# An earlier request for half of w1, and two places in TensorE's first plan

## The chip, the cores and the metric

The kernel runs on one core of a Trainium2 chip. The metric is the device time of one execution in microseconds (us), as the median of several runs. The profile tells of one further execution, taken by the hardware profiler.

## The reference

The reference is a block-sorting attention followed by a mixture of experts.

```python
# attention: 4 batches, 8 heads, 768 rows of 64, in 8 blocks of 96 rows
for _ in range(5):                        # P = sort_net, (4, 8, 8, 8)
    P = exp(P - max(P, -1)); P /= sum(P, -1) + 1e-9; P /= sum(P, -2) + 1e-9
k_sorted = einsum('bhij,bhjcd->bhicd', P, k_blocks)     # v_sorted likewise
scores = q_block @ k_sorted_block.T / sqrt(64)          # inside each block
out = softmax(scores) @ v_sorted_block
# experts: x is that output as 3072 rows of 512; 8 experts, hidden width 1024
P = exp(x @ w_gate - max)
for _ in range(8):
    P /= P.sum(1) + 1e-9; P /= P.sum(0) + 1e-9; P *= 3072 / 8
out = sum_e P[:, e] * (relu(x @ w1[e]) @ w2[e])
```

## The kernel before

**Stages.** The first batch's attention runs by itself at the start. The attention of batches two to four is woven with expert 0 of the batch ahead, and the other seven experts follow. Matrix products run on TensorE in bf16 with f32 sums. ScalarE and VectorE empty its banks, GpSimd issues the loads that turn f32 into bf16 and does sums that need no bank.

**The sort.** P is balanced in five rounds, spread over 128 partitions, and multiplied with a mask into R (`Rt[bb]`), a 128 x 128 matrix for each head. `sort_values` (L144) multiplies R with the values, copies the products to `vs` and moves them to `vsbt` with eight transfers, one a block of rows (`vsb` in the profile). For the first batch block i goes out on SP, GpSimd and ScalarE in turn, so SP has blocks 0, 3 and 6. `keys` (L186) sorts the keys in the same way. R of the first batch is made on VectorE. R of the second batch is made on GpSimd by `build_r` (L130), in two instructions of four heads each, line L134.

**w1 of expert 0.** It is loaded in two halves by `half_w1` (L103): half 0 holds rows 0 to 255 of w1, so kk = 0 and 1 of the four steps over the inner dimension; half 1 holds kk = 2 and 3. Half 0 is asked for early. Half 1 is asked for on GpSimd between the two R instructions of the second batch (L461 to L464). Behind it GpSimd asks for the second batch's v, k and q and for w2 of expert 0 (L465, L466).

**The order of the work.** `pin` is the language's request to keep an instruction in the order in which the program names it. Everything on TensorE and GpSimd is pinned, and so is nearly all of the first batch on ScalarE and VectorE. The first batch's order is written out by hand in the string `PLAN0`, which `first_attention` (L306) walks through. A letter is a step, the first digit is the pair of heads, the second the half of the blocks:

- `k0`: sort the keys of pair 0 (L194, copies on VectorE L200). `s00`: scores of pair 0, half 0 (L218), and their exponentials on ScalarE (L232).
- `d00`: denominators, a product of the exponentials with ones (L243), and their reciprocal on VectorE (L246). `m00`: the mix with the sorted values (L256) and a multiply by the reciprocal on VectorE (L258). With a capital letter (`D`, `M`) the VectorE part is put off until a step `f`.
- `t00`: turn the result (L282) and copy it to `xtT` (L287), the input of the experts.
- `w2`: two matmuls into a bank that nobody reads (`unread`, L423).
- `e0`: the first two of eight pieces of expert 0's hidden layer, kk = 0 and 1, in two banks (L358). `e1` is kk = 2, `e2` is kk = 3 and the relu. So e1 is the first reader of half 1 of w1. `h0`: a further piece of the hidden layer (L368). `l0`, `l3`: logits (L300).

**The banks.** The first stage takes its results from seven banks. Which bank a step gets is settled when the program is built: the one that comes free first. So a step can have to wait for whoever reads the bank's earlier content.

Of the kernel before, what the change touches and what calls it, by code (L numbers as in the profile page):

```python
# [20 lines left out]
def mkap(t, dims, off=0):  # L21
    return bass.AP(tensor=t.tensor, offset=t.offset + off, ap=dims)
# [3 lines left out]
def kernel(  # L26
# [11 lines left out]
    nc = tc.nc  # L38
# [33 lines left out]
    def load_batch(bb, parts):  # L72
        for d, name in ((vt, "vt"), (kt, "kt"), (qt, "qt")):
            d[bb] = kvp.tile([128, 8, 384], BF16, name=name, bufs=2)
        load_rest(bb, parts)
# [16 lines left out]
    def load_w2(e):  # L92
        w2t[e] = (wq if e else wcp).tile([128, 8, Dm], BF16, name="w2e")
        pin(nc.gpsimd.dma_start(out=w2t[e],
                                in_=moe_w2[e].rearrange("(fb k) f -> k fb f", k=128)))
# [7 lines left out]
    def half_w1(h):  # L103
        pin(nc.gpsimd.dma_start(
            out=w1t[0][:, 2 * h:2 * h + 2],
            in_=moe_w1[0, 256 * h:256 * h + 256].rearrange("(kk k) f -> k kk f", k=128)))
# [23 lines left out]
    def build_r(bb, eng, n):  # L130

        Rt[bb] = perp.tile([128, 8, 8, 16], BF16, name=f"R{bb % 2}")
        for h in range(0, 8, n):
            ins = eng.tensor_tensor(  # L134
                out=mkap(Rt[bb], [Rt[bb].ap[0], [16, 8 * n], [1, 16]], off=h * 128),
                in0=mkap(Pb, [Pb.ap[0], [1, 8 * n], [0, 16]], off=(bb * 8 + h) * 8),
                in1=mkap(mask16, [mask16.ap[0], [0, 8 * n], [1, 16]]),
                op=ALU.mult)
            if eng is nc.gpsimd:
                pin(ins)  # L140
            yield


    def sort_values(bb, bank, n=8, h0=0):  # L144
        for h in range(h0, n):
            vps = bank([128, 384], F32)
            pin(nc.tensor.matmul(vps, Rt[bb][:, h].rearrange("p i c -> p (i c)"),  # L147
                                 vt[bb][:, h, :], start=True, stop=True))
            (nc.vector.tensor_copy if bb == 0 and h in (3, 5, 7) or bb == 1 and h % 2 else
             nc.scalar.copy)(  # L150
                vs[:, :, h, 0:64], vps.rearrange("p (kk d) -> p kk d", d=64))
            if h % 2:
                yield

        for i in range(NB if n == 8 else 0):
            eng = ((nc.sync, nc.gpsimd, nc.scalar)[i % 3] if bb == 0 else
                   nc.gpsimd if i % 2 else nc.sync)
            (pin if bb == 0 else lambda ins: ins)(eng.dma_start(
                out=mkap(vsbt[bb % 2], [[VW, 96], [1, 520]], off=i * 520),
                in_=vs[16 * i:16 * i + 16].rearrange("p kk h d -> p kk (h d)")))  # L160
# [3 lines left out]
    def queries(bb, hp, bank):  # L164

        qps = bank([128, 6, 128], BF16)
        if bb < 2:

            for kk in range(6):
                for h in range(2):  # L170
                    pin(nc.tensor.matmul(qps[64 * h:64 * h + 64, kk, :],
                                         qt[bb][:, 2 * hp + h, kk * 64:kk * 64 + 64],
                                         Ibig, is_transpose=True, start=True, stop=True))
        else:
            qr = sp.tile([128, 6, 2, 64], BF16, name="qr", bufs=2)
            nc.gpsimd.tensor_copy(
                qr.rearrange("p kk h d -> p h kk d"),
                qt[bb][:, 2 * hp:2 * hp + 2].rearrange("p h (kk d) -> p h kk d", d=64))
            for kk in range(6):
                pin(nc.tensor.matmul(qps[:, kk, :], qr[:, kk].rearrange("p h d -> p (h d)"),  # L180
                                     Ibig, is_transpose=True, start=True, stop=True))
        qT[bb, hp] = sp.tile([128, 128, 6], BF16, name="qTs", bufs=4)
        (pin if bb == 0 else lambda ins: ins)(
            nc.scalar.copy(qT[bb, hp], qps.rearrange("p kk c -> p c kk")))

    def keys(bb, hp, bank):  # L186

        kT[bb, hp] = sp.tile([128, NB, 16, 6], BF16, name="kTs")
        for b in range(2):
            kps = bank([128, 3, 128], F32)  # L190
            for j in range(3):
# [11 lines left out]
    at = {}  # L203
    ATP = 12
    order = pin
    PLAN0 = ("k0 k1 w3 s00 s01 k2 w2 s10 k3 w2 s20 d00 d01 s30 d10 d20 s11 s21 d30 m00 m10 m20 m30 "
             "t00 D11 t10 M01 t20 D21 s31 t30 f3 e0 e1 m11 e2 m21 t01 h0 d31 t11 h0 m31 h0 t21 h0 "
             "h0 t31 h0 l0 l3")

    def scores(bb, hp, bank, halves=(0, 1)):  # L210
# [95 lines left out]
    def first_attention(bank, warm, fill):  # L306
# [13 lines left out]
              "h": lambda n: next(fill), "w": warm}  # L320
        for x in PLAN0.split():
            do[x[0]](*(int(c) for c in x[1:]))
# [40 lines left out]
    def expert_hidden(c0, hTs, bank):  # L363
        n = 384
        for fb in range(2 if c0 == 0 else 0, 8):
            hps = bank()
            for kk in range(4):
                pin(nc.tensor.matmul(hps[:, 0:n], w1t[0][:, kk, fb * 128:(fb + 1) * 128],  # L368
                                     xtT[:, kk, c0:c0 + n], start=(kk == 0), stop=(kk == 3)))
            if c0 == n and fb % 2:  # L370
                nc.vector.tensor_scalar_max(hTs[:, fb, 0:n], hps[:, 0:n], 0.0)
            else:
                (order if c0 == 0 else lambda ins: ins)(
                    nc.scalar.activation(out=hTs[:, fb, 0:n], in_=hps[:, 0:n], func=AF.Relu))
            yield
# [38 lines left out]
    with tc.tile_pool(name="ps0", bufs=7, space=bass.MemoryType.PSUM,  # L414
                      reuse_waits="tile") as ps0, \
            tc.tile_pool(name="psw", bufs=1, space=bass.MemoryType.PSUM) as psw:
        bank0 = lambda shape, dt: ps0.tile(shape, dt, name="bank", tag="bank")
        unread = psw.tile([128, 4, 128], F32)

        def warm(n):  # L420

            for _ in range(n):
                pin(nc.tensor.matmul(unread, Ibig, mkap(Ibig, [Ibig.ap[0], [0, 4], [1, 128]]),  # L423
                                     start=True, stop=True))

        nc.vector.reduce_max(out=rs, in_=P, axis=AX.X)
        nc.vector.tensor_sub(P, P, mkap(rs, [rs.ap[0], rs.ap[1], [0, 8]]))
        for it in range(5):
            pin(nc.scalar.activation(out=P, in_=P, func=AF.Exp))
            if it >= 2:  # L430
                queries(0, it - 2, bank0)
            if it == 3:
                warm(4)
            nc.vector.reduce_sum(out=rs, in_=P, axis=AX.X)
            nc.vector.reciprocal(out=rs, in_=rs)
            nc.vector.tensor_mul(P, P, mkap(rs, [rs.ap[0], rs.ap[1], [0, 8]]))
            nc.vector.reduce_sum(out=cs, in_=Pt, axis=AX.X)
            if it == 0:
                nc.vector.tensor_scalar_add(cs, cs, 1e-9)
            nc.vector.reciprocal(out=cs, in_=cs)  # L440
            nc.vector.tensor_mul(Pt, Pt, mkap(cs, [cs.ap[0], cs.ap[1], [0, 8]]))
        for eng, i0, n in ((nc.vector.tensor_copy, 0, 5), (nc.scalar.copy, 5, 3)):
            (pin if i0 else lambda ins: ins)(
                eng(Prep[:, i0:i0 + n], mkap(P, [P.ap[0], [8, n], [1, 8], [0, 16]], off=i0 * 8)))
        queries(0, 3, bank0)
        warm(3)
        pbps = bank0([128, 8, 32], F32)
        for i in range(8):
            pin(nc.tensor.matmul(pbps[:, i, :], Prep[:, i].rearrange("p j c -> p (j c)"),
                                 Ibig[0:32, 0:32], start=True, stop=True))  # L450
        Rt[0] = perp.tile([128, 8, 8, 16], BF16, name="R0")
        for h in range(0, 8, 2):
            nc.vector.tensor_tensor(
                out=Rt[0][:, h:h + 2],
                in0=mkap(pbps, [pbps.ap[0], [1, 2], [32, 8], [0, 16]], off=h),
                in1=mkap(mask16, [mask16.ap[0], [0, 2], [0, 8], [1, 16]]), op=ALU.mult)
        warm(4)
        for _ in sort_values(0, bank0):
            pass
        nc.scalar.copy(Pb, pbps.rearrange("p i g -> p g i"))  # L460
        half = build_r(1, nc.gpsimd, 4)  # L461
        next(half)
        half_w1(1)
        next(half, 0)  # L464
        load_batch(1, [("v", 0, 8)] + [(x, l0, 4) for l0 in (0, 4) for x in "kq"])  # L465
        load_w2(0)  # L466
        def tiles():
            yield from expert_hidden(0, begun[0], lambda: bank0([128, 512], F32))

        first_attention(bank0, warm, tiles())  # L470
# [359 lines left out]
    for m, o in enumerate(ends):  # L830
        e, p, hT, _ = chunks[-1]
# [84 lines left out]
```

## Time and profile before

| what | value |
|---|---|
| median of 3 runs | 672.54 us (672.49 to 672.54) |
| the profiled execution | 673.19 us |
| its span, first to last instruction | 671.40 us |
| granted TensorE clock, mean | 0.999 |
| busy: TensorE / VectorE / ScalarE / GpSimd | 97% / 70% / 57% / 70% |
| HBM read / written | 52.45 MB / 6.29 MB |

The profiled execution is 1.79 us longer than its span: this much lies before the first and behind the last instruction. Times in the views count from the span's start. A line names the engine, the line of the kernel, the operation, the tile that is written and those that are read, and in brackets the idle time ahead and what ended it. `PE` is TensorE, `PEld` its weight loads, `DVE` VectorE, `ACT` ScalarE, `POOL` GpSimd, `SP` SyncE. Matmuls are pipelined, so their durations overlap; the distance from start to start tells what one costs.

### The profile page before, as it was taken

The numbers are of one execution on the slowest core, as the hardware profiler recorded it, in microseconds if no ns is written. First come the engines' busy times: TensorE is split into PE (matmuls) and PEld (weight loads), VectorE is DVE, ScalarE is ACT, GpSimd is POOL, SyncE is SP. The second block draws the span as 40 slices with busy tenths as digits, with TensorE's granted clock in tenths as the row PEclk, the third lists the DMA queues.
The fourth block names the chain that finished last, engine by engine and source line by source line (L and its number), as shares of the span: only waits on it lengthen the run. The fifth ranks groups of instructions, "written<-read, shape, count | busy, mean of one in ns | idle before, by whom it ended". The sixth has DMA issues, their size and how long they took to land.

```text
span 671.4 us, 13342 instructions
## 1 busy us (share of the span) xinstructions
PE 653.3 (97%) x5096; PEld 435.3 (65%) x5174; DVE 471.7 (70%) x967; ACT 380.0 (57%) x736; POOL 469.7 (70%) x438
## 2 busy tenths in 40 slices
PE   5999999999999999999999999999999999999997
PEld 3766666654566666666666666666666666666665
DVE  6665547667677777777777777777777777777775
ACT  4684646466777755555555645555555555555540
POOL 3542741086979998779796969789697969846641
PEclk9999999999999999999999999999999999999999
DMA  9999962103040212030403030211303040000224
GB/s 153 179 216 150 148 106 36 30 1 62 1 63 9 56 21 44 1 62 1 64 1 63 1 63 2 44 21 15 49 1 63 1 63 1 1 1 35 92 85 168
DMA packets 31985, 36.59 MB, mean 54 GB/s; under 512 B 2032, under 2 KB 24400, under 8 KB 31920
## 3 DMA queue, kind: packets, MB, share of 16 engines
q0 software_dynamic: 25840, 27.72, 25.9%
q1 hardware_dynamic: 5856, 7.82, 4.0%
q8 instruction: 40, 0.66, 0.4%
q10 hardware_dynamic: 224, 0.20, 0.1%
q14 instruction: 25, 0.20, 0.1%
HBM read 52.45 MB, written 6.29 MB: 87 GB/s over the span
## 4 chain that ended last, share of the span: by engine, by line
PE 89%; POOL 4%; DVE 2%; issue 2%; DMA 2%; ACT 1%; DVEq 0%; POOLq 0%; ACTq 0%
PE oacc L738 37%; PE bk L627 34%; PE bank L381 5%; PE bank L368 4%; POOL hs L728 1%; DMA w1e<-in_moe_w_dram 1%; PE bank L270 1%; PE bk L704 1%; POOL wc L411 1%; PE bk L795 1%; PE bank L218 1%; PE bank L194 1%; PE bank L282 1%; PE bank L147 1%; PE bk L803 1%
## 5 line engine op out<-in xcount | busy, mean ns | idle before, releaser
L688 DVE SCALAR_TENSOR_TENSOR osbl<-oacc,glog,osbl 128x256 f32<-128x256 f32 (+1 forms) x410 | 219.1, 535 | 127.5 <-PE oacc L738 118.0
L613 ACT ACTIVATE hT<-bk 128x512 bf16<-128x512 f32 (+1 forms) x176 | 104.2, 592 | 148.6 <-PE bk L627 131.4
L627 PE MATMUL bk<-xtT,w1e 128*128 128x512 bf16 x478 | 143.5, 379 | 0.9
L738 PEld LDWEIGHTS <-hs 128*128 128x128 bf16 x984 | 96.2, 98 | 63.2 <-POOL hs L728 0.5
L738 PEld LDWEIGHTS <-hT 128*128 128x128 bf16 x904 | 88.4, 98 | 59.0 <-issue 1.8
L728 POOL TENSOR_TENSOR hs<-hT 128x512 bf16<-128x512 bf16 x82 | 94.7, 1155 | 36.0 <-DVE hT L616 30.6
L738 PE MATMUL oacc<-w2e,hT 128*128 128x256 bf16 x764 | 114.6, 273 | 0.7 <-DVE osbl L688 0.3
L728 POOL TENSOR_TENSOR hs<-hs,hT 128x512 bf16<-128x512 bf16 x82 | 94.6, 1154 | 6.4
L728 POOL TENSOR_TENSOR hs<-hT,hs 128x512 bf16<-128x512 bf16 x82 | 94.6, 1153 | 6.4
L627 PE MATMUL bk<-xc,wc 128*128 128x512 bf16 x317 | 95.2, 379 | 0.1
L738 PE MATMUL oacc<-w2e,hs 128*128 128x256 bf16 x616 | 92.4, 273 | 0.7
L627 PEld LDWEIGHTS <-w1e 128*128 128x128 bf16 x672 | 65.8, 98 | 11.7 <-issue 0.5
L616 DVE CUSTOM_DVE_ANT_0 hT<-bk,p 128x512 bf16<-128x512 f32 x84 | 58.1, 691 | 7.9 <-PE bk L627 3.1
L662 ACT COPY p<-bk 128x512 f32<-128x512 f32 x84 | 49.2, 585 | 25.0 <-PE bk L627 22.0
L656 ACT COPY u<-bk 128x512 f32<-128x512 f32 x84 | 49.2, 586 | 22.2 <-PE bk L627 19.5
L647 ACT COPY bk<-bk 128x512 f32<-128x512 f32 x84 | 48.0, 572 | 20.5 <-PE bk L627 20.5
L616 DVE CUSTOM_DVE_ANT_0 hT<-bk,u 128x512 bf16<-128x512 f32 x84 | 57.0, 678 | 1.0 <-PE bk L627 0.6
L738 PE MATMUL oacc<-w2s,hs 128*128 128x256 bf16 x368 | 55.2, 273 | 0.3
L627 PEld LDWEIGHTS <-wc 128*128 128x128 bf16 x504 | 49.3, 98 | 8.0 <-issue 0.2
L681 DVE SCALAR_TENSOR_TENSOR s<-bk,hT 128x512 bf16<-128x512 f32 x80 | 54.4, 680 | 0.0
L627 PE MATMUL bk<-xtT,wc 128*128 128x512 bf16 x160 | 48.2, 379 | 0.4
L627 PE MATMUL bk<-xc,w1e 128*128 128x512 bf16 x158 | 47.8, 379 | 0.1
(148 smaller groups left out, 851.8 us busy)
## 6 DMA issues: line engine op xcount, KB each, us to landing
w2e<-in_moe_w_dram POOLq DMA_DIRECT2D x8, 1024.0 KB, 9.3
w1e<-in_moe_w_dram POOLq DMA_DIRECT2D x7, 1024.0 KB, 8.1
out_dram<-osbl SPq DMA_DIRECT2D x23, 256.0 KB, 2.0
vt<-in_v_dram POOLq DMA_DIRECT2D x3, 768.0 KB, 11.6
qt<-in_q_dram POOLq DMA_DIRECT2D x4, 384.0 KB, 10.5
kt<-in_k_dram POOLq DMA_DIRECT2D x4, 384.0 KB, 12.3
kt<-in_k_dram POOLq DMA_DIRECT2D x2, 768.0 KB, 14.4
qt<-in_q_dram POOLq DMA_DIRECT2D x2, 768.0 KB, 17.4
```

Of the source, the lines that this page charges most:

```text
L368: pin(nc.tensor.matmul(hps[:, 0:n], w1t[0][:, kk, fb * 128:(fb + 1) * 128], xtT[:, kk, c0:c0 + n], start=(kk == 0), stop=(kk == 3)))
L381: pin(nc.tensor.matmul(oacc, hTs[:, fb, tt * 128:(tt + 1) * 128], w2t[0][:, fb, :], start=(fb == 0), stop=(fb == 7)))
L613: relu = lambda o, x: nc.scalar.activation(out=o, in_=x, func=AF.Relu)
L616: return nc.vector._custom_dve(TENSOR_ADD_SAT, out=o, in0=x, in1=y, s0=TOP, s1=0.0)
L627: pin(nc.tensor.matmul(ps, wa[:, kk, :], xa[:, kk, :], start=(first and kk == 0), stop=(kk == 1), skip_group_check=True))
L647: pin(nc.scalar.copy(t["w"], t["u"]))
L656: pin(nc.scalar.copy(t["u2"], t["u"]))
L662: pin(nc.scalar.copy(t["p5"], t["v"]))
L681: pin(nc.vector.scalar_tensor_tensor(out=s3[:, i, :], in0=t["w"], scalar=0.0, in1=c12, op0=ALU.max, op1=ALU.subtract))
L688: pin(nc.vector.scalar_tensor_tensor(out=o, in0=ps, scalar=glog[:, t, e:e + 1], in1=o, op0=ALU.mult, op1=ALU.add))
L728: pin(nc.gpsimd.tensor_tensor(out=s[:, c], in0=a, in1=b, op=o))
L738: pin(nc.tensor.matmul(ps, h[:, fb, :], w[:, fb, :], start=(first and fb == 0), stop=(fb == 3), skip_group_check=True))
```

## The change

Three things move, and one matmul goes.

- Half 1 of w1 is asked for ahead of both R instructions of the second batch, where it stood between them.
- In `PLAN0`, `d00` moves from behind `s20` to ahead of it, and the second `w2` becomes `w1`: one unread matmul instead of two.
- In `PLAN0`, `s31`, the scores of the last pair's second half, moves from ahead of `t30` to behind `e0`.

```diff
-    PLAN0 = ("k0 k1 w3 s00 s01 k2 w2 s10 k3 w2 s20 d00 d01 s30 d10 d20 s11 s21 d30 m00 m10 m20 m30 "
-             "t00 D11 t10 M01 t20 D21 s31 t30 f3 e0 e1 m11 e2 m21 t01 h0 d31 t11 h0 m31 h0 t21 h0 "
+    PLAN0 = ("k0 k1 w3 s00 s01 k2 w2 s10 k3 d00 w1 s20 d01 s30 d10 d20 s11 s21 d30 m00 m10 m20 m30 "
+             "t00 D11 t10 M01 t20 D21 t30 f3 e0 s31 e1 m11 e2 m21 t01 h0 d31 t11 h0 m31 h0 t21 h0 "
              "h0 t31 h0 l0 l3")
...
         nc.scalar.copy(Pb, pbps.rearrange("p i g -> p g i"))
-        half = build_r(1, nc.gpsimd, 4)
-        next(half)
         half_w1(1)
-        next(half, 0)
+        for _ in build_r(1, nc.gpsimd, 4):
+            pass
         load_batch(1, [("v", 0, 8)] + [(x, l0, 4) for l0 in (0, 4) for x in "kq"])
```

## Prediction

> **What bounds the kernel now.** First the page's part on the chain that ended last:
>
> ```profile
> PE 89%; POOL 4%; DVE 2%; issue 2%; DMA 2%; ACT 1%; DVEq 0%; POOLq 0%; ACTq 0%
> ```
>
> TensorE's own order sets the time; what counts is where it stands still. Next the chain of waits over the first 45 us (start, us, what):
>
> ```profile
> 17.02 1.61 POOL vsb L158 x3
> 18.63 1.00 POOL R L134
> 19.63 9.10 DMA w1e<-in_moe_w_dram
> 28.77 0.50 PE bank L358 x2
> ```
>
> GpSimd issues three transfers of the sorted values, builds half of the second batch's sort matrices R, and only then asks for the second half of w1. That half lands at 28.73, and step e1 waits for it. From 28.77 the chain is TensorE's but for ScalarE from 43.5 to 45.5, VectorE's routing steps between 142 and 158 and GpSimd's sums from there to 185, each of which starts behind a result of TensorE. What is won or lost ahead of e1 is thus carried to the end, unless a transfer holds it up again.
>
> TensorE's timeline around both edited places of the plan (start, busy us, line, tile, count):
>
> ```profile
> 19.16 0.53 PE L194 MATMUL bank<-R,kt 128*64 128x128 bf16 x12
> 19.61 0.61 PE L423 MATMUL unread<-Ibig 128*128 128x512 bf16 x2
> 20.15 0.38 PE L218 MATMUL bank<-qTs,kTs 64*96 64x96 bf16 x8
> 20.46 0.91 PE L243 MATMUL bank<-one,atp 96*96 96x64 bf16 x16
> 21.29 0.38 PE L218 MATMUL bank<-qTs,kTs 64*96 64x96 bf16 x8
> ...
> 26.92 0.94 PE L358 MATMUL bank<-xtT,w1e 128*128 128x384 bf16 x4
> 28.77 0.34 PE L358 MATMUL bank<-xtT,w1e 128*128 128x384 bf16 x1 [0.91 <-DMA w1e<-in_moe_w_dram]
> ```
>
> Between 26.92 and 28.77 only four matmuls ran. The first two start at 26.92 and 27.09; the other two at 27.38 and 27.54, since their bank was that of s31's first scores, whose exponential ended at 27.33. TensorE was free for e1 at 27.70: it stood 1.07 us.
>
> GpSimd's timeline, then the table by stretches (length, then busy us of TensorE, weight loads, VectorE, ScalarE, GpSimd, then clock, DMA share, GB/s):
>
> ```profile
> 18.62 1.09 POOL L134 TENSOR_TENSOR R<-Pb,mask 128x512 bf16<-128x512 f32 x1
> 19.63 0.77 POOL L104 DMA_DIRECT2D w1e<-in_moe_w_dram  x1
> 20.41 1.07 POOL L134 TENSOR_TENSOR R<-Pb,mask 128x512 bf16<-128x512 f32 x1
> 21.41 0.95 POOL L80 DMA_DIRECT2D vt<-in_v_dram  x1
> ```
>
> ```profile
> 22.00:24.00 2.00, 2.00 (x52) 1.91 (x50) 0.74 (x4) 1.72 (x6) 2.00 (x4) 1.00 0.83 139
> 24.00:26.00 2.00, 2.00 (x50) 2.00 (x48) 2.00 (x4) 1.31 (x4) 2.00 (x3) 1.00 0.92 126
> 26.00:28.70 2.70, 1.86 (x28) 1.12 (x25) 1.49 (x5) 1.46 (x4) 0.23 (x1) 1.00 1.12 152
> 28.70:40.00 11.30, 11.23 (x124) 7.76 (x124) 6.44 (x14) 6.49 (x14) 0.00 (x0) 1.00 1.30 201
> ```
>
> The transfers run below the 201 GB/s that they reach afterwards, and what is missing from 22.0 to 28.7 is 2 x 62 + 2 x 75 + 2.7 x 49 = 406 KB, about 2.0 us at 201 GB/s. So there is idle transfer time that an earlier request could use; whether the request is what is late there, no row says.
>
> Last the DMA issues by narrow windows (us to landing): the sorted values' second on SP, issued 17.17; the half, issued 19.63; and SP's last of the second batch, issued 42.00 behind w2's megabyte.
>
> ```profile
> vsb<-vs SPq DMA_DIRECT2D x1, 97.5 KB, 5.9
> w1e<-in_moe_w_dram POOLq DMA_DIRECT2D x1, 512.0 KB, 9.1
> vsb<-vs SPq DMA_DIRECT2D x1, 97.5 KB, 7.4
> ```
>
> **The request.** It moves past one R instruction: issue at 18.63 instead of 19.63. Its 0.77 us on GpSimd now precede both R instructions (1.00 + 1.07 by their starts), so vt, k, q and w2 are asked for from 21.41 as before, in the same order; SP's and ScalarE's issues keep their places. R's first half is done about 0.8 us later, at 20.5; its reader, the second batch's sort, starts at 36.0, so that costs nothing. What the landing gains is not shown; bounds: 0 (the sorted values ahead of it in the queue land at 23.0 on GpSimd and 23.84 on SP, and the half needs only 512 KB / 201 = 2.6 us of transfer, so something other than its own bytes already takes time) and 2.0 (all the idle transfer time). I take 1.0, the shift of the issue: landing 27.73.
>
> **d00 ahead of s20, one unread matmul less.** By start distances the old order takes 0.54 (two unread) + 0.31 (s20) + 0.83 (d00, d01) = 1.68. An unread matmul less is -0.22 (their start distance inside the run of four from 13.11); splitting d00 from d01 adds one change of kind, 0.05 to 0.10. So s30 starts at 21.14, 0.15 earlier. s20 itself starts about 0.20 later, 20.35; ScalarE stood 0.40 ahead of its exponential, so the exponentials end at 21.63, and d20, then at about 21.87, still finds them. d00 reads scores exponentiated at 18.64; its reciprocal keeps its place behind k3's copies. The clock stays at 1.00 through these stretches; d00 fills the place of the matmul that goes.
>
> **s31 behind e0.** Nothing is added. Carrying the 0.15: D21 25.84, t30 26.28 (its mixed values come from a VectorE multiply that ended at 26.35, now 26.20), e0 26.46, whose banks no longer hang on s31: 0.65 for four matmuls, so the 0.13 us wait at 27.38 goes. s31 27.11, e1 ready at 27.42. s31's exponentials end near 28.4; their reader d31 came 2.2 us behind e1 and still comes after 29.5. VectorE's and ScalarE's orders are unchanged.
>
> **Sum.** e1 starts at the later of 27.42 and 27.73 + 0.04 = 27.77, instead of 28.77: -1.00. The next place that can take it back is the second batch's first mix: SP's last rows land 42.00 + 7.38 = 49.38, and the matmul that reads them starts at 49.42. These transfers are issued when that batch's sort ends, so 1.0 earlier too, but share the engines with w2. Give-back 0 to 1.0; I take 0.1, since the half and all behind it move up into the idle transfer time. Net -0.9: span 671.40 to 670.5, the profiled execution 673.19 to 672.3 (1.79 lie around the span), and the median, 0.65 below that execution, 672.54 to 671.6. The bound for a difference is 0.2%, 1.35 us, about what a measurement of this kernel can tell from no change.
>
> **A rule against it.** The row: SP's transfers of these values took 4.6 to 5.9 us to land in the first batch, 7.1 to 7.4 with w2 queued beside them, 3.1 in the third batch. The Trainium skill, "DMA: Bandwidth & Descriptors", section "Queues, rings and completion order", says that each DMA engine takes turns between the queues that have work, a packet at a time. By that rule the half, ready earlier, takes turns with SP's last sorted values and delays them while it gains itself; the trace agrees as far as 5.9 against 7.4 goes. With SP's rows later by that difference the sum would be no gain at all (rival three).
>
> **Rivals.**
> One: the landing moves up by 1.3 or more and the request was what left the transfers idle. Then TensorE decides: e1 at 27.42, -1.35 with rounding, and the stream behind it is early enough for the mixes at 48.97, whose 16 matmuls took 1.06 to the next start against 0.71 for the later groups. 1.35 plus half of these 0.35 gives -1.5: 671.0. For: 2.0 us idle transfer time. Against: only 1.0 us of issue is moved.
> Two: hidden. The half queues behind the sorted values whatever its issue, or 49.38 stays and takes the gain back. 672.4. For: vt, asked for at 21.41, is not earlier. Against: the missing 406 KB.
> Three, slower: SP's second transfer carries block 3 for m00, whose fourth matmul would come at 23.29, 0.19 behind the landing at 23.10. A later landing stalls TensorE there. It is slower than before once the landing is late by 0.19 + 1.35 = 1.5 us. With 7.4 instead of 5.9 it is just even; behind the whole half's 2.6 us it is +1.1, and behind the half's landing at 27.7 it is 4.4 - 1.35 = +3.1. Taken nearer to the first: +1.4, 673.9.
>
> **How the numbers follow.** Forecast 0.37, rival one 0.30, two 0.13, three 0.20. Rival one lies beyond the bound and gives faster 0.30; the forecast and two lie within, 0.50; three beyond on the other side, 0.20. The range runs from 670.7 (rival one with all 0.35, and 0.1) to 674.4 (three, short of its far end); the forecast's own is 671.2 to 672.4.
>
> **What would show it.** GpSimd's issue at 18.63, landing near 27.7, e1 at 27.8 with a wait of 0.3 or none; e0's matmuls evenly spaced; the first batch's mixes starting near 23.15 without a wait; the mix at about 48 without one. The step on the landing is wrong if the half lands after 28.3 or before 27.4; the sum is wrong if m00 waits for vsb, or if the second batch's mixes still start at 49.

## The result: slower by 0.28%, and the profile after

| | before | after |
|---|---|---|
| median of 22 runs each | 672.88 us (672.13 to 674.50) | 674.82 us (671.76 to 677.83) |
| ratio of after to before | | 1.0028 [1.0017, 1.0038] |
| profiled execution | 673.19 us | 676.03 us |
| its span | 671.4 us | 674.3 us |
| its mean granted clock | 0.999 | 0.997 |

The prediction was 671.6 us in a range of 670.7 to 674.4. It was wrong: the time lies above the range, on the side of rival three.

First the page's part on the chain that ended last, now with twice the share for transfers, and the chain of waits up to 28.6 us (start, us, what), both of the kernel after.

```profile
PE 87%; POOL 4%; DMA 4%; issue 2%; ACT 1%; DVE 1%; SPq 0%; DVEq 0%; POOLq 0%; ACTq 0%
```

```profile
17.22 0.97 SPq L158
18.25 9.90 DMA vsb<-vs
28.15 0.04 issue
28.19 0.41 PE bank L256 x6
```

The half of w1 is no longer in the chain. In its place stands SP's third transfer of the first batch's sorted values, block 6. It is issued at 18.25 and needs 9.90 us. Before, it was issued at 18.13 and landed at 23.84, after 5.7 us. Its first reader is M01, the mix of pair 0, second half. The DMA issues and TensorE's timeline of the kernel before show both, M01 without a wait:

```profile
vsb<-vs SPq DMA_DIRECT2D x1, 97.5 KB, 5.7
```

```profile
25.44 0.51 PE L256 MATMUL bank<-vsb,atp 96*96 96x88 bf16 x8
```

GpSimd's timeline of the kernel after shows the request at the predicted place, and what is behind it where it was:

```profile
18.65 0.77 POOL L104 DMA_DIRECT2D w1e<-in_moe_w_dram  x1
19.40 2.11 POOL L134 TENSOR_TENSOR R<-Pb,mask 128x512 bf16<-128x512 f32 x2
21.41 0.94 POOL L80 DMA_DIRECT2D vt<-in_v_dram  x1
```

The DMA issues of the kernel after, by narrow windows (size, us to landing): the half, issued at 18.65, and SP's third.

```profile
w1e<-in_moe_w_dram POOLq DMA_DIRECT2D x1, 512.0 KB, 9.2
vsb<-vs SPq DMA_DIRECT2D x1, 97.5 KB, 9.9
```

The half lands at 27.88, 0.85 earlier than before, and block 6 at 28.15, 4.3 later. Each transfer is spread over 16 transfer engines, and by the trace's semaphore events all 16 shares of block 6 are late: the first of them lands at 23.84, when the last one had landed before (21.68 to 23.84 there).

TensorE's timeline of the kernel after (start, busy us, line, tile, count, and in brackets the idle time ahead and its releaser):

```profile
20.32 0.38 PE L218 MATMUL bank<-qTs,kTs 64*96 64x96 bf16 x8
20.63 0.55 PE L243 MATMUL bank<-one,atp 96*96 96x64 bf16 x8
21.10 0.38 PE L218 MATMUL bank<-qTs,kTs 64*96 64x96 bf16 x8
...
25.25 0.25 PE L256 MATMUL bank<-vsb,atp 96*96 96x88 bf16 x2
28.19 0.41 PE L256 MATMUL bank<-vsb,atp 96*96 96x88 bf16 x6 [2.69 <-DMA vsb<-vs]
...
30.42 0.82 PE L358 MATMUL bank<-xtT,w1e 128*128 128x384 bf16 x2
```

The first three lines are s20, d01 and s30: s30 starts at 21.10, against 21.29 before. After two matmuls of M01 TensorE stands for 2.69 us. Then e1 starts at 30.42, where it was 28.77: 1.65 later instead of 1.0 earlier.

That is not yet 2.9. The rest is in the table by stretches (length, then busy us and counts of TensorE, weight loads, VectorE, ScalarE, GpSimd, then granted clock, DMA share, GB/s). First after, then before for the second of its stretches:

```profile
26.00:28.70 2.70, 0.51 (x13) 0.51 (x12) 0.16 (x1) 0.00 (x0) 0.22 (x1) 1.00 1.12 170
29.80:33.10 3.30, 3.30 (x32) 2.51 (x32) 1.35 (x3) 1.74 (x4) 0.00 (x0) 0.50 1.31 201
```

```profile
29.80:33.10 3.30, 3.30 (x45) 2.58 (x44) 2.44 (x6) 1.85 (x4) 0.00 (x0) 1.00 1.30 201
```

After the stall the granted clock is 0.50 from 29.76 for 3.41 us. TensorE is busy all the time but does 32 matmuls where it did 45. Half of 3.41 is 1.7 us lost, some 0.3 of it ahead of e1's start. At the first turn of the second batch's queries the lag is 2.9 (42.91, before 40.01), and it stays so to the end of the span.

The Trainium skill, "TensorE: Matmul & The Clock Gate", Part 1, says that the clock falls to a half after an idle window of about 3.4 us, that the window runs freely, and that the effect varies from run to run. The trace agrees on the 3.41 us of half clock; but here a stand of 2.7 us was enough.

The runs differ in this. In 11 of the 22 runs of after the mean granted clock is 0.997 or lower, and their median is 676.03; the other 11 have a median of 673.1, 0.2 over before. Only one run, of the first 11, has a trace, so how late block 6 was in the others isn't known.

### The profile page after: what moved, and what is told of

It is laid out like the page before. It is cut to its first block, busy times and chain, and to the rows that moved or that the text cites. A ratio compares the mean times of both kernels' runs of the same rounds, so it can differ in the third digit from the quotient of the medians.

```text
span 674.3 us, 13340 instructions
## 1 busy us (share of the span) xinstructions
PE 654.7 (97%) x5095; PEld 436.3 (65%) x5173; DVE 471.5 (70%) x967; ACT 380.9 (56%) x736; POOL 469.8 (70%) x438
## 4 chain that ended last, share of the span: by engine, by line
PE 87%; POOL 4%; DMA 4%; issue 2%; ACT 1%; DVE 1%; SPq 0%; DVEq 0%; POOLq 0%; ACTq 0%
PE oacc L737 36%; PE bk L626 33%; PE bank L381 5%; PE bank L368 4%; POOL hs L727 2%; DMA vsb<-vs 1%; DMA w2e<-in_moe_w_dram 1%; PE bank L270 1%; PE bk L703 1%; POOL wc L411 1%; DMA qt<-in_q_dram 1%; PE bk L794 1%; PE bank L218 1%; PE bank L282 1%; PE bank L194 1%
```

## The experiments

Theory: the earlier request puts the half in front of, or level with, SP's sorted values on the transfer engines; their reader stalls, and the clock falls after the stall. Rivals: the new plan costs the time; or the request does, but through the half's own landing or through what is asked for behind it.

**One part of the change at a time.** e1_request has the old plan with the new place of the request; e2_plan has the new plan with the request between the two halves of R.

```diff
 e1_request, against before
-        half = build_r(1, nc.gpsimd, 4)
-        next(half)
         half_w1(1)
-        next(half, 0)
+        for _ in build_r(1, nc.gpsimd, 4):
+            pass
 e2_plan, against before
-    PLAN0 = (the old string)
+    PLAN0 = (the new string)
```

> The request alone: the half of w1 is asked for ahead of both R instructions, PLAN0 is that of before. Theory (turns): the half reaches the transfer engines while SP's third transfer of the sorted values (block 6) still waits there, and holds it back: block 6 lands at 27 to 28.2 instead of 23.84, the half at 27.9; M01 stands 2.5 us or more, the clock falls to half for 3.4 us in such a run, and the median is 1.5 to 3 us over before. Rival (plan): the two edits of the plan are what costs; then this one is no slower than before.

> The plan alone: PLAN0 of after, the half of w1 asked for between the R instructions as before. Theory (turns): block 6 lands near 23.8 and the half near 28.7, e1 starts at 28.8, no half clock, and the median is that of before within 0.5 us, since e1 waits for the half whatever TensorE has done. Rival (plan): about 1.9 us over before, with a stall at M01 or a low clock here too.

The request alone: median 673.95 against 672.85, ratio 1.0023 [1.0008, 1.0038]. The plan alone: 672.92 against 672.85, 1.0005 [0.9995, 1.0015]. So the request is what costs. What GpSimd asks for behind it didn't change: vt goes out at 21.41 before and after. The profiled execution of e1_request, 680.68 us, is the slowest of its 12 and its sorted values go out 0.8 us later than before; its stall is at m00. Its DMA issues show SP's second transfer, issued at 17.98, and TensorE's timeline shows the matmuls of m00:

```profile
vsb<-vs SPq DMA_DIRECT2D x1, 97.5 KB, 9.8
```

```profile
24.08 0.31 PE L256 MATMUL bank<-vsb,atp 96*96 96x88 bf16 x3
27.81 1.75 PE L256 MATMUL bank<-vsb,atp 96*96 96x88 bf16 x21 [3.42 <-DMA vsb<-vs]
```

```profile
28.00:38.10 10.10, 10.10 (x106) 8.57 (x104) 4.79 (x10) 3.17 (x7) 0.00 (x0) 0.50 1.31 202
```

Block 3 lands at 27.77 and block 6, issued only at 20.55, at 28.04; the half, issued at 19.40, lands at 27.58. m00 stands 3.42 us ahead of its fourth matmul, and the table's stretch behind it shows the clock at 0.50; it stays there for 10.24 us, three times the 3.41 of after. This is rival three at its far end, and some 5 us of clock (half of 10.24) on top of it. In after's profiled execution block 3 was in time and block 6 was held; here block 3 is held as well.

In e2_plan the expected gain is there as far as the plan goes: block 6 lands at 23.27 and nothing stands but e1, for the half that lands at 28.26.

```profile
28.31 0.50 PE L358 MATMUL bank<-xtT,w1e 128*128 128x384 bf16 x2 [0.67 <-DMA w1e<-in_moe_w_dram]
```

**Out of the way.** e3_six is after with block 6 moved from SP's queue to GpSimd's, where it is asked for ahead of the half.

```diff
-            eng = ((nc.sync, nc.gpsimd, nc.scalar)[i % 3] if bb == 0 else
+            eng = ((nc.sync, nc.gpsimd, nc.scalar)[1 if i == 6 else i % 3] if bb == 0 else
```

> After, with block 6 of the first batch's sorted values issued on GpSimd ahead of the half instead of third on SP. Theory (turns between queues): in GpSimd's own queue the half can't pass it; block 6 lands by 23.6, M01 doesn't stand, the clock stays at 1.00. GpSimd issues one more, 0.53 us, so the half is asked for at 19.2 and lands at 28.0 to 28.5; the time is 0.2 to 0.8 us under before. Rival (too little transfer rate for all of it by then): whatever queue block 6 is in, it or another block lands after 26 and the time stays 1 to 3 us over before.

Median 672.77 against 672.85, 1.0004 [0.9989, 1.0019]: the loss is gone, the gain isn't there. Block 6, issued on GpSimd at 18.20, lands at 23.43, and block 7 behind it at 23.70. The DMA issues of e3_six have the two in one line:

```profile
vsb<-vs POOLq DMA_DIRECT2D x2, 97.5 KB, 5.1
```

The half, issued at 19.20, lands at 27.64, and e1 starts at 27.68 without a wait, 1.09 ahead of before. TensorE's timeline of e3_six, with e1 and the second batch's first mix, and before's for the latter, show where this goes:

```profile
27.68 0.50 PE L358 MATMUL bank<-xtT,w1e 128*128 128x384 bf16 x2
...
47.87 0.82 PE L270 MATMUL bank<-vsb,atp 96*96 96x65 bf16 x6
49.06 0.59 PE L270 MATMUL bank<-vsb,atp 96*96 96x65 bf16 x10 [0.38 <-DMA vsb<-vs]
49.49 1.03 PE L381 MATMUL bank<-w2e,hTs 128*128 128x512 bf16 x4
```

```profile
48.97 1.19 PE L270 MATMUL bank<-vsb,atp 96*96 96x65 bf16 x16
50.03 0.81 PE L381 MATMUL bank<-w2e,hTs 128*128 128x512 bf16 x2
```

The mix comes 1.1 earlier, and stands for SP's last sorted values of the second batch, which land at 49.02. L381 behind it is only 0.54 ahead, and the span 0.3 shorter (671.1).

**The clock by itself.** e4_fill is after with 12 matmuls that nobody reads ahead of M01, where TensorE stood.

```diff
-    "t00 D11 t10 M01 t20 ..."
+    "t00 D11 t10 w9 w3 M01 t20 ..."
```

> After, with twelve unread matmuls (about 2.6 us) on TensorE just ahead of M01, where it stood idle. Theory: block 6 lands at 28.1 all the same and M01 goes on at 28.2, but TensorE was busy, so the granted clock stays at 1.00 through 29 to 33; of after's 2.9 us in the profiled execution some 1.7 go, and 1.0 to 1.4 over before remain. Rival (the low clock isn't due to the stall, or costs nothing): clock 0.5 there again or the time of after unchanged.

Median 674.51 (674.01 to 679.25) against 672.85, 1.0029 [1.0015, 1.0043]. The profiled execution has block 6 nearly as late as after, at 27.62 against 28.15. TensorE's timeline and the table of e4_fill:

```profile
25.39 2.75 PE L423 MATMUL unread<-Ibig 128*128 128x512 bf16 x12
27.98 0.51 PE L256 MATMUL bank<-vsb,atp 96*96 96x88 bf16 x8
```

```profile
28.00:33.00 5.00, 5.00 (x79) 3.98 (x78) 2.97 (x9) 2.71 (x6) 0.00 (x0) 1.00 1.30 198
```

With TensorE at work the clock stays at 1.00, and the span is 672.8, 1.4 over before. So by these two executions some 1.4 of after's 2.9 is the stand and 1.5 the clock. The median is no better. The lowest run is 674.01, where after has runs down to 671.76, so it seems that the 12 matmuls are paid for in each execution, also where block 6 would have been early. The mean clock is 0.997 or lower in 1 of 10 runs here, 5 of 12 of e1_request, 0 of 12 of e2_plan, 1 of 11 of e3_six and 1 of 35 of before beside them. So it is frequent where the request is early and SP has block 6 with nothing filling the gap, and rare elsewhere; that each such run had a stand is not shown.

**Does the half land by its request?** e5_late is before with the half asked for behind both R instructions, at 20.65. e6_quarters is after with the half as two requests of 128 rows.

```diff
 e5_late, against before
-        half = build_r(1, nc.gpsimd, 4)
-        next(half)
-        half_w1(1)
-        next(half, 0)
+        for _ in build_r(1, nc.gpsimd, 4):
+            pass
+        half_w1(1)
 e6_quarters, against after
+    def quarter_w1(kk):
+        pin(nc.gpsimd.dma_start(out=w1t[0][:, kk], in_=moe_w1[0, 128 * kk:128 * kk + 128]))
...
-        half_w1(1)
+        quarter_w1(2)
+        quarter_w1(3)
```

> Before, with the half of w1 asked for behind both R instructions, 1.0 us later. Theory (the time of the request sets who goes first): block 6 lands at 23.3 to 24 as before, M01 doesn't stand, and the half lands 0 to 1.0 later, 28.7 to 29.7; e1 moves by that and the time is 0 to 1.0 us over before, without half clocks. Rival (the slow block 6 is chance and not the request's): block 6 lands after 27 in a run here too, with 2 us or more lost.

> After, with the second half of w1 asked for in two requests of 128 rows, one for each kk. Theory (a transfer engine serves its whole share of one request, 16 rows of the half, before it turns to SP's queue): with 8 rows a request it turns sooner, block 6 lands at 25 to 26.5 instead of 28.15, M01 stands 0 to 1.2 us, and the time lies within 0.7 us of before. Rival (it divides by bytes, whatever the requests): block 6 lands at 28 and the time is that of after, about 2 us over before.

e5_late: 673.08 against 673.03, 0.9995 [0.9969, 1.0021]. Its DMA issues and TensorE's timeline:

```profile
w1e<-in_moe_w_dram POOLq DMA_DIRECT2D x1, 512.0 KB, 7.8
```

```profile
28.52 0.50 PE L358 MATMUL bank<-xtT,w1e 128*128 128x384 bf16 x2 [0.68 <-DMA w1e<-in_moe_w_dram]
```

Asked for 1.0 later than before, the half lands at 28.48, not later than 28.73. The landing doesn't follow the request in these executions. Block 6 lands at 23.32, so it isn't held.

e6_quarters: 675.13 (672.41 to 677.5) against 673.03, 1.0028 [1.0010, 1.0047]. The time was expected within 0.7 us of before and is 2.1 over; the mechanism shows in its DMA issues (the two quarters in one line, then SP's third):

```profile
w1e<-in_moe_w_dram POOLq DMA_DIRECT2D x2, 256.0 KB, 8.1
vsb<-vs SPq DMA_DIRECT2D x1, 97.5 KB, 8.7
```

```profile
26.92 0.41 PE L259 MATMUL bank<-vsb,atp 96*96 96x88 bf16 x6 [1.27 <-DMA vsb<-vs]
```

The quarters land at 26.32 and 27.70, block 6 between them at 26.88, and M01 (L259 here) stands 1.27 us. This execution has a span of 672.2 and no half clock. But 6 of its 12 runs have the low mean clock, so one profile speaks for the better half of them only.

The Trainium skill, "DMA: Bandwidth & Descriptors", section "Queues, rings and completion order", says that a transfer engine takes turns between queues and empties a whole packet of one before it turns to the next. Block 6 that lands with the half (28.15 and 27.88), and between the quarters when there are two, agrees with that.

How close the two requests are matters too. Nine profiled executions have block 6 on SP. In the five in which the half was asked for 1.4 to 2.5 us behind it (before, e2_plan, e5_late, e8_w2, e11_hold) block 6 took 4.8 to 5.7 us; in the three with 0.4 to 0.5 us (after, e4_fill, e6_quarters) it took 8.7 to 9.9. e1_request doesn't fit: its block 3 was issued 1.4 ahead of the half and took 9.8.

**What lies ahead or behind.** e11_hold is e2_plan with R of the second batch computed three times, so that v, k, q and w2 are asked for from 25.73 instead of 21.41. One execution of it is on record, 673.51 us.

```diff
         next(half, 0)
+        for _ in range(2):
+            for _ in build_r(1, nc.gpsimd, 4):
+                pass
         load_batch(1, ...)
```

> The plan of after with the half asked for between the R instructions, and the second batch's R computed three times over, so that v, k, q and w2 are asked for 4 us later, from about 25.6. It asks what the half's landing hangs on, since moving its request by 1.0 us either way moved it little. If the requests behind it slow it, it lands at 25 to 26.5; if what lies ahead of it does, it lands at 27.2 to 28.7 as in the other runs.

The half, issued at 19.65, lands at 28.39 all the same (8.7 us). The table of e11_hold shows how little else the transfers do towards the end:

```profile
24.00:26.00 2.00, 2.00 (x50) 2.00 (x48) 2.00 (x4) 1.24 (x4) 2.00 (x3) 1.00 0.72 123
26.00:28.70 2.70, 1.75 (x25) 1.10 (x23) 1.27 (x5) 1.31 (x3) 2.70 (x4) 1.00 0.58 57
```

So in this execution the requests behind it aren't what makes the half late. Between 26.0 and 28.7 only 57 GB/s move, and it still lands no sooner.

**The give-back.** Four runs go at the second batch's last sorted values. e7_six_w2 is e3_six with w2 of expert 0 as two requests, the second behind those values; e8_w2 is before with w2 split in that way; e9_w2_six is e7_six_w2 with the second batch's block 6 on GpSimd; e10_six_six is e3_six with that block on GpSimd and w2 whole. e12_again repeats e10_six_six. The three runs with w2 in two requests also pin the second batch's transfers to their order.

```diff
 e7_six_w2, e8_w2, e9_w2_six
-        load_w2(0)
+        half_w2(0)
...
             (behind sort_values of the second batch)
+                half_w2(1)
...
-            (pin if bb == 0 else lambda ins: ins)(eng.dma_start(
+            (pin if bb < 2 else lambda ins: ins)(eng.dma_start(
 e9_w2_six, e10_six_six, e12_again
-                   nc.gpsimd if i % 2 else nc.sync)
+                   nc.gpsimd if i % 2 or bb == 1 and i == 6 else nc.sync)
```

> The kernel with block 6 on GpSimd, and w2 of expert 0 asked for in two halves, the second one behind the second batch's sorted values. Theory (what that kernel gained at e1 was taken back at the second batch's first mix by transfers behind w2): the second batch's sorted values land by 47, that mix doesn't stand, and the time is 0.8 to 1.3 us under before. Rival (something else holds the mix): the mix still stands until 49 or a later wait takes its place; the time is that of before within 0.3 us.

> Before, with only w2 of expert 0 asked for in two halves as in the kernel with block 6 on GpSimd. Theory: the mix at 48.97 loses its short waits, 0.2 to 0.4 us under before; e1 still starts at 28.8. Rival: w2's second half is late for its reader at 51.9 and the time is over before.

> The kernel with block 6 on GpSimd and w2 in two halves, and now the second batch's block 6 on GpSimd too, ahead of w2's second half. Theory (SP's last transfer is held back by whatever large request GpSimd has ready just behind it): the second batch's sorted values all land by 46.5, where SP's last took until 49.45; the mix at 47.9 doesn't stand; what is left is the wait for the third batch's v near 54, 0.6 us or less; 0.3 to 1.0 us under before. Rival (the rate of all transfers together binds there): the mix or the third batch's sort gives all of it back, the time is that of before or above it.

> The kernel with block 6 on GpSimd, and the second batch's block 6 on GpSimd too, w2 in one request as before. Theory: SP's last of the second batch no longer waits behind the third batch's v; all its sorted values land by 48.9 instead of 49.02 at most, since GpSimd's stand behind w2 anyway: 0 to 0.3 us under the kernel with block 6 alone. Rival: GpSimd's fifth lands later than SP's did and the time rises by 0.5 or more.

> The kernel with both batches' block 6 on GpSimd once more, since its ratio of 0.9994 to before had an interval that holds 1. Theory (e1's wait is gone and nothing takes it back): again 0.3 to 0.6 us under before, no run with a half clock. Rival (no gain): the median within 0.2 us of before or above it.

| run | median, us | before | ratio |
|---|---|---|---|
| e7_six_w2 | 674.58 | 673.03 | 1.0031 [1.0016, 1.0045] |
| e8_w2 | 674.44 | 673.03 | 1.0029 [1.0012, 1.0047] |
| e9_w2_six | 675.15 | 672.74 | 1.0036 [1.0024, 1.0049] |
| e10_six_six | 672.36 | 672.74 | 0.9994 [0.9985, 1.0003] |
| e12_again | 672.51 | 672.88 | 0.9994 [0.9985, 1.0003] |

Splitting w2 failed, in e7_six_w2 in line with the mechanism under study: SP's last values of e7_six_w2, issued at 41.01, land at 49.45, while GpSimd's last, in the queue that also carries w2's second half behind them, land at 46.18. The DMA issues and TensorE's timeline of e7_six_w2:

```profile
vsb<-vs SPq DMA_DIRECT2D x1, 97.5 KB, 8.4
```

```profile
49.49 0.59 PE L277 MATMUL bank<-vsb,atp 96*96 96x65 bf16 x10 [0.99 <-DMA vsb<-vs]
```

In e8_w2 and e9_w2_six the mix is on time, but w2's second half now lies ahead of the third batch's v, and that batch's sort (L154) waits 0.98 us in the one and in e9_w2_six

```profile
55.77 0.48 PE L154 MATMUL bank<-vt,R 128*128 128x384 bf16 x2 [1.92 <-DMA vt<-in_v_dram]
```

With w2 whole and both blocks on GpSimd, nothing stands. TensorE's timeline of e10_six_six:

```profile
27.57 0.50 PE L358 MATMUL bank<-xtT,w1e 128*128 128x384 bf16 x2
...
47.77 1.19 PE L270 MATMUL bank<-vsb,atp 96*96 96x65 bf16 x16
48.83 1.02 PE L381 MATMUL bank<-w2e,hTs 128*128 128x512 bf16 x3
```

e1 is 1.20 ahead of before and L381 still is. The span is 670.3, 1.1 shorter, near the 0.9 that the prediction summed for the change alone. In the medians 0.37 and 0.38 of it are left, and each interval holds 1. It is the fastest version here, but not shown to be faster than before; none of its 23 runs has a mean clock of 0.997 or below.

## Why the prediction was wrong

- **GpSimd's order and the plan: right.** The request is at 18.65 (forecast 18.63) and vt at 21.41. s30 starts at 21.10 (21.14) and s20 at 20.32 (20.35). The plan alone costs nothing (e2_plan). d00 and d01 apart take 0.39 and 0.47 by start distances, 0.03 more than the 0.83 of both together, where the sum had 0.05 to 0.10. With the half early enough, e1 starts at 27.57 in e10_six_six, 0.15 behind the forecast 27.42; 0.10 of that is e0, whose four matmuls took 0.75 and not 0.65.
- **"I take 1.0, the shift of the issue": near in number, by luck.** The half gained 0.85 in after. But e5_late moved the request 1.0 the other way and lost nothing, and in 13 profiled executions whose requests lie between 18.65 and 20.65 the half lands between 26.8 and 29.1, in no order with them; with the request at 18.78 in e4_fill it landed at 29.11. The reason for the bound 0, that something other than the half's own bytes takes time, was the better guide. The 406 KB of "idle transfer time" were read from the GB/s alone; the DMA share beside them was 0.83 to 1.12, against 1.30 at 201 GB/s, so by that column the transfer engines had 64 to 86% of their later load there.
- **The request's price for others: this step failed.** The sum put it at nothing: SP's transfers kept their issues, and it was taken that they keep their landings. The runs showed a landing 4.3 us later for block 6, and 2.7 us of stand at M01. The text had the mechanism as rival three and gave it 0.20. It let the rule of turns weigh with "7.4 instead of 5.9", came out "just even" at one end, and ended its range short of the other. The runs showed 9.9 and 9.8: held for as long as the half itself, the far end of rival three. "SP's second" for m00 is what e1_request shows; after shows SP's third for M01. That one had landed 1.6 ahead of its reader before, and the sum gave it no line. A transfer that can move by 4.3 us needs every reader of its queue in the sum.
- **"The clock stays at 1.00": right only without a stall.** No rival had a price for the clock behind a stand. It is some 1.5 of the 2.9 us, by e4_fill.
- **"Give-back 0 to 1.0; I take 0.1": mis-sized.** e3_six gained 1.09 at e1 and kept 0.54 at L381: some 0.55. The place that the text named, SP's last rows of the second batch, was the right one.
- **What it would have brought.** With block 6 of both batches out of SP's queue, e10_six_six has a span of 670.3 against the forecast 670.5. That the two agree is in part luck: the half, asked for at 19.11, landed at 27.02 and not 27.73, and the give-back was removed by an edit of its own.

What stays open: why the half lands at 26.8 to 29.1 whatever its request. The trace's semaphore events show the 16 transfer engines finishing their shares of it 3 to 4 us apart (24.69 to 27.88 in after, 24.93 to 28.73 before), but not what holds the late ones back. It is also open why block 3 is held in one profiled execution and not in the other, and whether either was in the 11 runs of after with a full clock.

## What to carry to other kernels

An earlier request of a large load is not free for small transfers that other queues have already issued: price each of them that was issued shortly ahead, with its first reader, as landing with the load. In this kernel the small transfer was safer ahead of the load in the load's own queue. And a stand of TensorE of 2.7 us was followed here by 1.7 us lost to the granted clock, one of 3.4 us by some 5, so a gain of 1 us isn't worth the risk of such a stand.

## What the runs showed of the hardware

- A transfer issued 0.4 us ahead of the half on another queue landed 0.27 us behind it: 9.9 us for 97.5 KB, against 5.7 before, with the half issued 1.5 us behind it. In GpSimd's own queue ahead of the half it landed at 23.43 (e3_six).
- A stand of 2.7 us was followed by 3.41 us of clock 0.50, one of 3.4 us by 10.24 us of it; stands of 1.27 us (e6_quarters) and 1.92 us (e9_w2_six) were followed by none. With unread matmuls in the gap the clock stayed at 1.00.
- 512 KB of w1 landed 7.8 us after the request at 20.65 and 9.2 us after that at 18.65, both near 28.
